# Seven block products in place of eight for the second feed-forward product of eight token groups, with a new instruction order

## The chip, the core and the metric

The kernel runs on one core of one Trainium2 chip. A core has a matrix engine (TensorE, PE in the profile, with its weight loads shown as PEld), a vector engine (VectorE, DVE), an activation engine (ScalarE, ACT), a general engine (GpSimd, POOL) and a queue engine that issues transfers (SyncE, SP). They run side by side and wait for each other through semaphores; each works through its own instructions strictly in the order in which they were written. Matrix products land in PSUM, in banks of 512 f32 values per partition; everything else is in SBUF. The metric is the device time of one execution in microseconds (us).

## What is computed

```
attention, B=4, H=8, S=768, D=64:
  keep = (column < 8) or (0 <= row - column < 96)
  scores = q k^T / 8 + (-slope[h] * distance), -1e9 where not kept
  x = softmax(scores) v, laid out as 3072 tokens x 512
feed-forward:
  h = x @ w_in                      (3072 x 2048)
  g = max(h,0) + log1p(exp(-|h|))   (softplus)
  out = g @ w_out                   (3072 x 512, f32)
```

## The kernel before

**Tiling.** The 3072 tokens are 24 blocks of 128 (`blocks`); attention works on one block `n`, the feed-forward part on a group `g` of two blocks, 256 tokens, so there are 12 groups. Matrix operands are bf16 in SBUF, sums are f32 in PSUM.

**Names of the operations.** Each step is an operation with a name, an engine, what it reads and what it writes; from these, `Program.op` (L27) derives what it waits for. For unit `i` (two blocks): `ldq/ldk/ldv` load f32 rows into a raw buffer, `castq/castk/castv` make bf16 copies, `trq/trk` transpose (on PE for units 0 to 2, by a transposing transfer from SP afterwards). For block `n`: `sc` scores (PE, L661), `z` bias (DVE, L687), `ex` exponential (ACT, L694), `pv` product with v (PE, L713), `nm` division (DVE, L724 and L725), `xt` transposition (PE or SP), `gk/gv` copies of the eight global rows. For group `g`: `a{g}.{p}`, p = 0 to 7, is product 1, eight matmuls of 256 columns (PE, L771) into one of two banks `h_ps`; `e` (ACT, L786) and `ln` (ACT, L797) make softplus into `g_t`; `b{g}.{ns}.{x}` is product 2 (PE, L820), per block `ns` 16 matmuls of 512 columns in four pieces of four; `oc` copies the PSUM bank to `osb` (DVE or ACT, L849) and `st` stores it (L852).

**Weights.** `win0` to `win7` and `wout0` to `wout7` (L429) are loads of 512 KB each of w_in and w_out; `cin` and `cout` (L431) cast them. `a{g}.6` and `a{g}.7` need the casts of win6 and win7.

**Raw buffers.** All loads share a ring of 12 raw buffers (`raw_slot`, L365), so a load waits for the casts of the load twelve places earlier. SP issues loads, transposing transfers and stores in one queue.

**Banks.** Eight: four of `s_ps`, two of `h_ps`, and `x_ps` and `o_ps` with one each. Product 2 uses `o_ps` except where `O_KEYS` and `LAST_KEYS` name another.

**What sets the order.** `ORDER` (L67) is one long list of names with their engines. It is followed as it stands: an engine gets its operations in the sequence in which they appear there. The numbers for durations and ranks at the `op` calls change nothing in what is run. `fill0` to `fill34` (L933) are 35 matmuls on zeros, whose result nothing uses.

Of the kernel before, what the change touches and what calls it, by code (L numbers as in the profile page):

```python
# [1 line left out]

# [65 lines left out]
blank:V table:A ones:G ldk0.0:S ldq0.0:A ident:G fill0:P ldk0.1:S ldq0.1:A fill1:P iota:G fill2:P ldv0:S fill3:P  # L68
ldq1.1:S dl0a:V fill4:P dl1a:V ldk1.0:S dl0b:V fill5:P dl1c:V fill6:P ldk1.1:S dl0c:V fill7:P dl1e:V d0:G fill8:P
castk0.0:A d0e:V ldv1:S fill9:P biasTrue0:V biasFalse7:A ldq1.0:S biasTrue5:V fill10:P biasTrue4:A biasTrue6:V  # L70
biasFalse3:A fill11:P biasTrue1:A win1:S biasFalse6:V castq0.1:G biasFalse5:A fill12:P win3:S castq0.0:A castk0.1:G
biasFalse1:A biasTrue3:A trq0.0:P biasFalse4:G biasTrue2:A trk0.0:P win0:S cpq0.0:A biasFalse0:G fill13:P fill14:P
cpk0.0:A fill15:P win2:S castq1.1:V fill16:P biasFalse2:A fill17:P cpq0.1:V cpk0.1:A fill18:P castk1.0:G win4:S
sb0.0:P biasTrue7:A castv0.10:V fill19:P castv0.00:G castv0.11:A sc0.0:P castk1.1:V sb1.1:P ex0.0:A sc1.1:P
castv0.01:G ex0.1:A sb1.0:P sc1.0:P ex1.1:A fill20:P pv0.0:P fill21:P ex1.0:A fill22:P castv1.00:G nm0.0:V trk1.0:P
fill23:P castq1.0:V pv0.1:P castv1.11:A fill24:P castv1.01:V pv1.1:P win5:S cpk1.0:A fill25:P nm0.1:V win7:S
trq1.0:P cpk1.1:A cin1:G nm1.1:V win6:S fill26:P fill27:P cpq1.0:A xt0:P pv1.0:P cpq1.1:A fill28:P ldk2.1:S nm1.0:V
castv1.10:A sc2.0:P ldk2.0:S xc0:A gv4.0:V fill29:P fill30:P z2.0:V xt1:P cin0:G fill31:P xc1:A z2.1:V sc3.0:P
gv4.1:A fill32:P cin3:G a0.1:P z3.0:V ex2.0:A ex2.1:A pv2.0:P cin2:G a0.0:P ldq2.1:S e0.1:A nm2.0:V ldq2.0:S ex3.0:A
gk4:G pv2.1:P sc3.1:P nm2.1:V a0.3:P e0.0:A cin4:G wout0:S z3.1:V ln0.0:A xt2:P a0.2:P cin5:G wout2:S e0.3:A xc2:V  # L80
pv3.0:P e0.2:A fill33:P a0.5:P wout1:S cin7:V ex3.1:A nm3.0:V a0.4:P e0.5:A wout3:S cin6:V pv3.1:P fill34:P e0.4:A
castk2.1:G nm3.1:V ldv2:S a0.7:P ln0.1:A castk2.0:G wout4:S a0.6:P castq2.1:V e0.7:A ln0.2:A xt3:P castq2.0:V
trk2.0:P xc3:V trq2.0:P e0.6:A a1.1:P cout0:G cpq2.0:V cpk2.0:A cpk2.1:A a1.0:P cpq2.1:V e1.1:A wout5:S cout2:V
sc4.0:P e1.0:A a1.3:P ln1.0:A z4.1:V cout1:G a1.2:P e1.3:A z4.0:V ex4.1:A b1.0.0:P ldq3:S b1.0.2:P ldk3:S a1.5:P
e1.2:A wout6:S gk5:V gv8.1:V ln1.1:A wout7:S b0.0.0:P castv2.00:G castv2.01:V sc5.0:P ex4.0:A b0.0.2:P z5.0:V a1.4:P
cout3:G ln0.3:A pv4.0:P castv2.11:G b0.0.4:P ldk4:S e1.5:A nm4.0:V sc5.1:P ldv3:S cout5:G e1.4:A b1.0.4:P z5.1:V
ex5.0:A pv4.1:P b0.0.6:P castv2.10:G b1.0.6:P gv5.0:G nm4.1:V a1.6:P castq3.0:A cout4:V b0.1.0:P gv5.1:A trq3:S
xt4:P a1.7:P castk3.11:G castk3.00:A xc4:A b0.1.2:P ex5.1:A b0.1.4:P cout6:G pv5.0:P b0.1.6:P gk6:A nm5.0:V e1.6:A
b0.0.8:P castk3.10:G ln1.2:A b0.0.10:P b0.1.8:P castk3.01:G b0.1.10:P e1.7:A cout7:G trk3:S pv5.1:P ln1.3:A
b0.1.12:P nm5.1:V b1.0.8:P b1.0.10:P castk4.00:V ldq4:S b0.0.12:P ldv4:S b0.1.14:P xt5:P castv3.11:G castv3.10:A  # L90
b1.0.12:P xc5:V castk4.01:A b1.0.14:P castk4.11:V castk4.10:A b0.0.14:P oc0.1.0:V a2.0:P gv6.0:A gv8.0:V oc0.0.0:A
st0.1.0:S a2.1:P castv3.00:V e2.0:A gk8:V oc1.0.0:V sc6.0:P e2.1:A a2.2:P castv3.01:A z6.1:V castq4.0:G b1.1.0:P
ldk5:S e2.2:A a2.3:P z6.0:V gv6.1:G st0.0.0:S ex6.1:A trk4:S a2.4:P e2.3:A gk7:G b1.1.2:P ex6.0:A trq4:S b1.1.4:P
sc7.0:P ln2.0:A ldq5:S a2.5:P z7.1:V e2.4:A pv6.0:P b1.1.6:P ldv5:S e2.5:A nm6.0:V b1.1.8:P ln2.1:A b1.1.10:P z7.0:V
# [12 lines left out]
sc12.0:P b3.1.4:P z12.0:V a4.4:P castv6.11:V castq7.0:V pv11.1:P b3.1.8:P e4.4:A z12.1:V trq7:S ln4.1:A nm11.1:V
b3.1.12:P xt11:S ex12.0:A a4.6:P ln4.0:A sc13.0:P st2.1.0:S oc3.1.0:A trk7:S a4.7:P ex12.1:A e4.6:A b4.0.0:P
st3.0.0:S e4.7:A pv12.0:P b4.0.4:P ln4.3:A nm12.0:V a5.1:P z13.1:V ln4.2:A a5.0:P e5.1:A z13.0:V b4.0.8:P ldq8:S
e5.0:A ex13.0:A pv12.1:P a5.3:P nm12.1:V b4.0.12:P xt12:S e5.3:A ex13.1:A a5.2:P oc4.0.0:V a5.5:P gk14:G ldk8:S  # L110
e5.2:A ln5.1:A pv13.0:P sc14.0:P ldv8:S nm13.0:V st4.0.0:S a5.4:P e5.5:A st3.1.0:S z14.0:V ln5.0:A pv13.1:P b4.1.0:P
nm13.1:V e5.4:A b4.1.4:P castq8.0:V xt13:S castk8.10:G castk8.11:A z14.1:V a5.6:P ex14.0:A gv14.0:G trq8:S b4.1.8:P
gv14.1:V castk8.00:G ex14.1:A b4.1.12:P gk15:A castk8.01:A a5.7:P oc4.1.0:V e5.6:A sc15.0:P castv8.10:V e5.7:A
a6.0:P b5.0.0:P ldq9:S e6.0:A ln5.2:A pv14.0:P a6.2:P nm14.0:V ln5.3:A z15.0:V a6.1:P ldk9:S pv14.1:P b5.0.4:P
e6.1:A nm14.1:V ln6.0:A a6.3:P castv8.00:V xt14:S z15.1:V e6.2:A b5.0.8:P ex15.0:A trk8:S gv15.1:V b5.0.12:P
gv15.0:V e6.3:A a6.4:P ex15.1:A oc5.0.0:V pv15.0:P castk9.01:V ln6.1:A a6.5:P nm15.0:V gk16:A castk9.00:V b5.1.0:P
castq9.0:A pv15.1:P e6.5:A b5.1.4:P nm15.1:V e6.4:A sc16.0:P gv16.0:V ln6.2:A xt15:S b5.1.8:P z16.1:V b5.1.12:P
st4.1.0:S trq9:S z16.0:V ex16.1:A a6.6:P ldv9:S a6.7:P oc5.1.0:A castk9.11:V gk17:G e6.6:A castk9.10:V gv16.1:G
# [964 lines left out]
```

## Time and profile before

| | |
|---|---|
| median of 3 runs (lowest, highest) | 216.16 us (216.04, 216.55) |
| the profiled execution: its time | 216.13 us |
| its span, first to last instruction | 214.2 us |
| PE, ACT, DVE, POOL busy | 208.3, 179.1, 117.9, 55.4 us |
| product 1 (L771), busy | 95.8 us |
| product 2 (L820) into `o_ps`, busy | 76.8 us |
| granted TensorE clock | 1.0 throughout |

The profiled execution takes 1.9 us more than its span; that lies around the span. The profile gives, for a group of instructions, the busy time, the mean length of one, and the idle time of the engine before them with what ended it. A matmul of a stream is pipelined: its own length (273 ns for 256 columns) is longer than the distance to the next, so a stream is priced from start to start.

### The profile page before, as it was taken

How to read it: one execution, taken by the hardware profiler on the slowest of the kernel's cores; microseconds unless marked ns; L12 is line 12 of the kernel's file. 1: busy time of each engine (PE TensorE's matmuls, PEld its weight loads, DVE VectorE, ACT ScalarE, POOL GpSimd, SP SyncE). 2: the span in 40 equal slices, each digit the busy share in tenths (PEclk: the TensorE clock that was granted, in tenths of full speed). 3: DMA queues.
4: the chain of work that ended last, by engine and by line, in shares of the span. 5: the costliest groups of instructions: out<-in, count | busy, mean ns of one | idle time of the engine just before them, and what ended most of it. 6: DMA issues, size and time to landing. Idle time of an engine off the chain costs nothing.

```text
span 214.2 us, 4986 instructions
## 1 busy us (share of the span) xinstructions
PE 208.3 (97%) x2003; PEld 142.3 (66%) x2003; DVE 117.9 (55%) x230; ACT 179.1 (84%) x263; POOL 55.4 (26%) x89
## 2 busy tenths in 40 slices
PE   7799999999999999999999999999999999999994
PEld 2466886657665878667767667767667666656753
DVE  5368787538587598736738575843675616300110
ACT  4999999989996998898889988998999598466651
POOL 3647435663071434300020012540043001000000
PEclk9999999999999999999999999999999999999999
DMA  5999999998999798965977679788486220300204
GB/s 190 338 378 388 387 364 341 340 230 248 239 286 194 175 233 194 178 141 167 214 194 205 67 176 230 163 215 190 135 206 78 63 98 20 105 25 3 98 0 148
DMA packets 69846, 40.95 MB, mean 191 GB/s; under 512 B 30144, under 2 KB 61248, under 8 KB 69824
## 3 DMA queue, kind: packets, MB, share of 16 engines
q1 hardware_dynamic: 69392, 40.05, 71.3%
q10 hardware_dynamic: 432, 0.59, 0.7%
q8 instruction: 15, 0.25, 0.5%
q14 instruction: 7, 0.06, 0.1%
HBM read 27.26 MB, written 6.29 MB: 157 GB/s over the span
## 4 chain that ended last, share of the span: by engine, by line
PE 90%; DMA 7%; SPq 1%; ACT 1%; POOL 0%; issue 0%
PE h_ps L771 40%; PE o_ps L820 31%; PE s_ps L820 6%; PE s_ps L661 5%; PE x_ps L713 4%; DMA raw<-in_moe_w_in_dram 4%; DMA raw<-in_v_dram 3%; PE x_ps L820 2%; SPq L388 1%; POOL w_in_bf L431 0%; PE o_ps L713 0%; PE s_ps L536 0%; ACT pb L694 0%; ACT vb L579 0%; PE o_ps L744 0%; PE x_ps L744 0%
## 5 line engine op out<-in xcount | busy, mean ns | idle before, releaser
L771 PE MATMUL h_ps<-XT,w_in_bf 128*128 128x256 bf16 x768 | 95.8, 273 | 0.0
L771 PEld LDWEIGHTS <-w_in_bf 128*128 128x128 bf16 x768 | 72.6, 98 | 17.0
L820 PE MATMUL o_ps<-w_out_bf,g 128*128 128x512 bf16 (+1 forms) x320 | 76.8, 371 | 0.0
L786 ACT ACTIVATE e<-h_ps 128x512 f32<-128x512 f32 x96 | 59.3, 630 | 15.5 <-PE h_ps L771 14.9
L820 PEld LDWEIGHTS <-g 128*128 128x128 bf16 x416 | 37.6, 98 | 29.8
L797 ACT ACTIVATE g<-e 128x1024 bf16<-128x1024 f32 x48 | 50.3, 1052 | 0.5
L687 DVE TENSOR_TENSOR z<-s_ps,biasA 128x1024 f32<-128x1024 f32 x38 | 45.7, 1219 | 6.6 <-PE s_ps L661 6.0
L694 ACT ACTIVATE pb<-z 128x1024 bf16<-128x1024 f32 (+1 forms) x44 | 43.0, 991 | 1.7 <-DVE z L687 1.5
L724 DVE RECIPROCAL rcp<-x_ps 128x4 f32<-128x4 f32 x40 | 7.2, 181 | 34.5 <-PE x_ps L713 34.2
L849 DVE COPY osb<-o_ps 128x512 f32<-128x512 f32 x13 | 9.0, 690 | 24.2 <-PE o_ps L820 24.1
L713 PEld LDWEIGHTS <-pb 128*128 128x128 bf16 x352 | 16.9, 98 | 6.1 <-ACT pb L694 0.5
L473 POOL CAST kb<-raw 64x512 bf16<-64x512 f32 x16 | 10.2, 637 | 38.8 <-DMA raw<-in_k_dram 23.5
L473 POOL CAST vb<-raw 64x512 bf16<-64x512 f32 x23 | 14.9, 646 | 15.5 <-DMA raw<-in_v_dram 13.5
L725 DVE TENSOR_TENSOR xs<-x_ps,rcp 128x256 bf16<-128x256 f32 x40 | 17.0, 424 | 1.4
L713 PE MATMUL x_ps<-vb,pb 128*128 128x65 bf16 x304 | 15.8, 193 | 0.0
L820 PE MATMUL s_ps<-w_out_bf,g 128*128 128x512 bf16 (+1 forms) x64 | 14.7, 352 | 0.0
L579 POOL COPY vb<-vb 4x512 bf16<-4x512 bf16 x12 | 7.9, 655 | 25.8 <-PE x_ps L713 25.2
L933 PE MATMUL x_ps<-blank 128*128 128x512 bf16 x35 | 11.5, 431 | 1.2 <-DVE blank L872 1.2
L661 PEld LDWEIGHTS <-kT 64*128 64x128 bf16 x224 | 6.8, 94 | 5.0 <-issue 4.9
L661 PE MATMUL s_ps<-qT,kT 64*128 64x128 bf16 x224 | 9.9, 218 | 0.0
L579 ACT COPY vb<-vb 4x512 bf16<-4x512 bf16 x10 | 6.1, 614 | 3.5 <-PE x_ps L713 3.4
L473 DVE CAST vb<-raw 64x512 bf16<-64x512 f32 x16 | 7.6, 474 | 1.1 <-DMA raw<-in_v_dram 0.8
(83 smaller groups left out, 129.7 us busy)
## 6 DMA issues: line engine op xcount, KB each, us to landing
raw<-in_v_dram SPq DMA_DIRECT2D x12, 512.0 KB, 5.6
out_dram<-osb SPq DMA_DIRECT2D x23, 256.0 KB, 2.6
raw<-in_q_dram SPq DMA_DIRECT2D x9, 512.0 KB, 4.6
raw<-in_k_dram SPq DMA_DIRECT2D x9, 512.0 KB, 5.0
raw<-in_moe_w_in_dram SPq DMA_DIRECT2D x8, 512.0 KB, 8.8
raw<-in_moe_w_out_dram SPq DMA_DIRECT2D x8, 512.0 KB, 8.1
raw<-in_k_dram SPq DMA_DIRECT2D x6, 256.0 KB, 6.3
raw<-in_q_dram SPq DMA_DIRECT2D x4, 256.0 KB, 7.6
```

The lines of the kernel that those rows point to most:

```text
L473: copy_on[eng](dst, src)
L579: copy_on[eng](vb_of(prev)[sl, :, 0:D], vb_of(first)[sl, :, 0:D])
L661: nc.tensor.matmul(reg if unit_of(n) in WIDE else reg.rearrange("p (r t) -> p r t", r=2), kt[rows, 2 * part + m, :], qv(rows, 2 * part + m ...
L687: nc.vector.tensor_tensor(z, src, bias, ALU.add)
L694: nc.scalar.activation(pb[:, 0:nr, :].rearrange("p (y a) b -> p y (a b)", y=2), src, AF.Exp, scale=1.0 / root_d)
L713: nc.tensor.matmul(xv[:, h, :], pb[:, 4 * (h % 2) + 2 * part + h // 2 if lone else u_all * (2 * (h % 2) + h // 2) + u, :], vb_of(prev if u ...
L725: nc.vector.tensor_tensor(xs[:, 4 * part : 4 * part + 4, :], xv[:, :, 0:D], rcp[:][:, :, None].to_broadcast([P, 4, D]), ALU.mult,)
L771: last = nc.tensor.matmul(hv[:, j, :], w_in_bf[:, m, fb * P : fb * P + P], XT[g % NXG][:, m, :], start=(m == 0), stop=(m == NM - 1),)
L786: nc.scalar.activation(e[:, p % 2, :, :].rearrange("p j (b t r) -> p (j b) r t", b=2, r=2), hb[:].rearrange("p (a r t) -> p a r t", a=4, r=2),
L797: nc.scalar.activation(gt[:, 2 * p - 2 : 2 * p + 2, :].rearrange("p a t -> p (a t)"), e[:].rearrange("p a j t -> p (a j t)"), AF.Ln, bias=1.0,
L820: nc.tensor.matmul(bank(key)[:, 0 : z - a], gt[:, fb, ns * P : ns * P + P], w_out_bf[:, fb, a:z], start=(fb == 0), stop=(fb == NFB - 1),)
L933: nc.tensor.matmul(x_ps[:], blank[:, 0:P], blank[:])
```

## The change

Product 2 of groups 4 to 11 is split into 2 x 2 blocks (128 tokens by 1024 features, times 1024 features by 256 outputs) and computed as Strassen's seven block products instead of eight. A11 to A22 are the four quarters of `g_t`; the sums of quarters are built on DVE or POOL (`ka`), the sums of w_out's blocks once (`ws`, 20 operations), and the seven products are put together on DVE while PSUM is emptied (`oe`). The sums of w_out read the f32 rows in the raw buffers of its one load. Eight raw buffers therefore hold w_out, two further ones are set aside, and the sums are kept in those two and in three of the eight; two more hold `ka` results. Three go back to the ring: from unit 3 on, loads go through 5 raw buffers instead of 12.

```
+FIRST_S = 4
+S_KEYS = {
+    10: {"3": ("o",), "4": ("o",), "5": ("x",), "2": ("x",), "1": ("s", 0, 0), "7": ("s", 1, 0), "6": ("s", 1, 0)},
+    11: {"3": ("o",), "4": ("o",), "5": ("x",), "2": ("x",), "1": ("s", 0, 0), "7": ("s", 1, 0), "6": ("h0",)},
+}
     def raw_slot(name):
-        raw_of[name] = len(raw_of) % NRAW
+        held = name[0] == "out"
+        if held and not spare:
+            spare.extend(idle.popleft() for _ in range(2))
+        raw_of[name] = idle.popleft()
+        if not held:
+            idle.append(raw_of[name])
...
+    def weight_sums(rank):
...
+        for p in range(4):
+            X, Y = (raw_t[at[x]][:].rearrange("p (a c) -> p a c", a=2) for x in (2 * p, 2 * p + 1))
...
+                ("6", X[:, :, lo], X[:, :, hi], ALU.add),
+                ("1", X[:, :, lo], Y[:, :, hi], ALU.subtract),
+                ("4", X[:, :, lo], Y[:, :, lo], ALU.add),
+                ("3", X[:, :, hi], Y[:, :, hi], ALU.add),
+                ("7", Y[:, :, lo], Y[:, :, hi], ALU.add),
...
+    def token_sums(g, rank):
...
+        for j, a, b in (("6", A21, A11), ("7", A12, A22), ("5", A12, A11), ("2", A21, A22), ("1", A11, A22)):
...
+                (nc.vector if eng == "DVE" else nc.gpsimd).tensor_tensor(dst, a[0], b[0], ALU.subtract)
...
+    def products(g, rank):
...
+        where = {"3": lo, "4": hi, "5": lo, "2": hi, "7": lo, "6": hi, "1": lo}
...
+            def fn(j=j, lhs=lhs, w=w):
+                for f in range(8):
+                    nc.tensor.matmul(psum(j), lhs[:, f // 2, f % 2, :], w(f), start=(f == 0), stop=(f == 7))
...
     def feed2(g):
+        if g >= FIRST_S:
+            token_sums(g, 16.0 * g + 16.0)
+            products(g, 16.0 * g + 17.0)
+            store_pair(g, 16.0 * g + 33.0)
+            return
```

`b{g}.3` to `b{g}.7` are the products, in the order 3, 4, 5, 2, 1, 7, 6 (3, 4, 5, 2, 1, 6, 7 in group 11, and 3, 5, 4, 2, 7, 6, 1 in group 10), each eight matmuls of 128 tokens by 256 columns. In groups 4 to 9 all seven use `o_ps`, two to the bank. `oe{g}.a` copies products 3 and 4 out (DVE or ACT); `oe{g}.b` is two subtractions of 256 columns, `oe{g}.c`, `.1` and `.7` are additions of 512 columns from PSUM to `osb`, in place (DVE). Group 11 has `.6` and `.7` apart, of 256 columns each, and stores its output in four quarters. `osb` becomes two buffers of 256 x 512 instead of three of 128 x 512.

`ORDER` is new as a whole, and with it the engines of many casts and copies. Of w_in and the units 1 and 2, this is the order on SP before and after:

```
-ldv0 ldq1.1 ldk1.0 ldk1.1 ldv1 ldq1.0 win1 win3 win0 win2 win4 win5 win7 win6 ldk2.1 ldk2.0 ldq2.1 ldq2.0 wout0
+ldq1.0 ldv0 ldq1.1 ldk1.0 ldk1.1 ldv1 win0 win1 win3 win2 ldq2.0 win4 win5 ldq2.1 win6 win7 ldk2.0 ldk2.1 wout0
```

The 35 `fill` matmuls stay. A stretch of the new order, with a hand-over of `o_ps` (`b4.2`, `oe4.b`, `oe4.c`, `b4.1`):

```
+e5.5:A b4.5:P z14.0:V gk15:A castk8.00:G e5.4:A b4.2:P xt13:S gv14.1:V gv14.0:G ex14.0:A a5.6:P oe4.b:V castv7.00:G
+ln5.2:A st3.1.0:S a5.7:P castk8.01:G oe4.c:V trq8:S e5.6:A castk8.11:G sc15.0:P castk8.10:V e5.7:A castv8.10:G
+pv14.0:P castv8.00:A b4.1:P castv8.11:V trk8:S ln5.3:A a6.0:P nm14.0:V ka5.6:G a6.1:P z15.1:V e6.0:A ldq9:S pv14.1:P
```

The other hunks adapt keys (`g_t` per quarter, `osb` per half) and the numbers at `op` calls, which nothing that runs depends on.

More of the change, by code (lines that the diff above doesn't have):

```diff
@@ L1 @@
 from contextlib import ExitStack
+from collections import deque
 import concourse.bass as bass
@@ L67 @@
 ORDER = """
[L68 to L82, printed above, removed]
@@ L143 @@
[L143 to L144 removed]
+blank:V ldq0.1:A iota:G ldk0.0:S fill0:P ldq0.0:A ldk0.1:S fill1:P dl0a:V fill2:P table:A ldq1.0:S dl1a:V dl0b:V
+fill3:P dl0c:V ldv0:S fill4:P dl1c:V d0:G ldq1.1:S dl1e:V fill5:P d0e:V fill6:P ldk1.0:S biasTrue4:A biasTrue7:A
+biasTrue0:V fill7:P biasFalse4:G biasTrue6:A biasTrue1:V castq0.1:A ldk1.1:S ones:G castk0.0:A biasFalse5:V ldv1:S
+ident:G biasFalse7:A biasFalse2:V biasFalse1:A win0:S castq0.0:A castk0.1:G win1:S biasFalse0:V biasTrue3:A trq0.0:P
@@ new lines, with ex @@
+    WSUM, c_t = {}, []
+    def weight_sums(rank):
+        at = {p: raw_of["out", p] for p in range(NSLOT)}
+        homes = spare + [at[0], at[1], at[2]]
+        lo, hi = slice(0, 256), slice(256, 512)
+        for p in range(4):
+            X, Y = (raw_t[at[x]][:].rearrange("p (a c) -> p a c", a=2) for x in (2 * p, 2 * p + 1))
+            xk, yk = raw_keys(at[2 * p]), raw_keys(at[2 * p + 1])
+            for z, (j, a, b, fn) in enumerate((
+                ("6", X[:, :, lo], X[:, :, hi], ALU.add),
[3 more added lines that the diff above has]
+                ("7", Y[:, :, lo], Y[:, :, hi], ALU.add),
+            )):
+                home, part = divmod(5 * p + z, 4)
+                slot = homes[home]
+                dst = raw_t[slot].bitcast(BF16)[:, 512 * part : 512 * part + 512].rearrange("p (a c) -> p a c", a=2)
+                WSUM[j, p] = dst
+                def ex(eng, dst=dst, a=a, b=b, fn=fn):
+                    (nc.vector if eng == "DVE" else nc.gpsimd).tensor_tensor(dst, a, b, fn)
+                op(f"ws{p}.{j}", "DVE", 0.0, rank, ex, reads={"6": xk, "7": yk}.get(j, xk + yk), writes=[("W", j, p)],
+                   port=True, after=[u for key in raw_keys(slot, (part // 2,)) for u in users(key)],
+                   alts={"DVE": 0.66, "POOL": 1.3})
+        for slot in (at[6], at[7]):
+            for x in range(2):
+                c_t.append((
+                    raw_t[slot].bitcast(BF16)[:, 1024 * x : 1024 * x + 1024].rearrange("p (i f t) -> p i f t", i=4, f=2),
+                    ("raw", slot, x),
+                ))
+        idle.extend((at[3], at[4], at[5]))
@@ new lines, in store_pair, with st @@
+    def store_pair(g, rank):
+        ob = osb_t[g % NOSB]
+        last = g == NGRP - 1
+        for tb, x in ((0, 1), (1, 0), (0, 0), (1, 1)) if last else ((0, None), (1, None)):
+            s, b = blocks[2 * g + tb]
+            t0 = S * s + P * b
+            cols = slice(0, DM) if x is None else slice(256 * x, 256 * x + 256)
+            queue = "ACT" if last and (tb, x) == (0, 0) else "SP"
+            def st(tb=tb, t0=t0, cols=cols, queue=queue):
+                return dma_on[queue].dma_start(out[t0 : t0 + P, cols], ob[:, tb, cols])
+            op(f"st{g}.{tb}.{x or 0}", queue, 0.4, rank, st, dma=(0.42, 60.0) if last else (0.72, 84.0),
+               reads=[("osb", g % NOSB, tb, y) for y in (range(2) if x is None else (x,))])
@@ L719, in pv @@
         reads = [("pb", at), "ones"] + v_keys(n) + (v_keys(prev) if i else [])
-        op(f"pv{n}.{part}", "PE", 0.29 if i else 0.15, rank, mm, reads=reads, writes=held([key]),
+        op(f"pv{n}.{part}", "PE", 0.237 if i else 0.12, rank, mm, reads=reads, writes=held([key]),
            count=8 if i else 4)
```

254 lines of the change are left out of this document (175 added, 79 removed).

## Prediction

> **What bounds the kernel now.** I read the page's busy times first, then the chain that ended last, then the stretches, then PE's rows by shape.
>
> ```profile
> PE 208.3 (97%) x2003; PEld 142.3 (66%) x2003; DVE 117.9 (55%) x230; ACT 179.1 (84%) x263; POOL 55.4 (26%) x89
> PE 90%; DMA 7%; SPq 1%; ACT 1%; POOL 0%; issue 0%
> ```
>
> PE is busy for 97% of the span, and 90% of the chain is PE after PE. Busy time alone proves little, since pipelined matmuls overlap, so I look at one long stretch and at the chain's pieces:
>
> ```profile
> 25.55:211.02 185.47, 185.46 (x1773) 127.94 (x1772) 102.53 (x188) 156.93 (x222) 42.10 (x64) 1.00 0.70 173
> ```
>
> ```profile
> 28.58 1.75 PE h_ps L771 x16
> 137.83 1.85 PE h_ps L771 x16
> 139.81 1.73 PE o_ps L820 x8
> ```
>
> The stretch (columns PE, PEld, DVE, ACT, POOL) shows PE without a gap from 25.55 to 211.02 us at full clock. In the chain, 16 matmuls of 256 columns take 1.75 us (0.11 each, 0.873 for an `a`), and 8 of 512 columns take 1.73 (0.216 each). Both run at one rate per column, so weight loads (98 ns in the rows by shape) hide even under 256 columns. The whole order on PE, priced like this (`sc` 0.553, `pv` 0.242, `fill` 0.216, from start to start), gives 183.1 us for this stretch against 185.5: 1.3% goes at changes between kinds of work. Hence time here is PE work, and what precedes 25.55 us.
>
> The start is bound otherwise (the timeline, then the stretches):
>
> ```profile
> 24.73 0.69 DVE L431 CAST w_in_bf<-raw 128x1024 bf16<-128x1024 f32 x1
> 25.55 1.91 PE L771 MATMUL h_ps<-XT,w_in_bf 128*128 128x256 bf16 x16
> ```
>
> ```profile
> 10.00:20.00 10.00, 9.72 (x124) 6.15 (x124) 7.24 (x18) 9.55 (x17) 6.02 (x8) 1.00 1.07 376
> 20.00:30.00 10.00, 10.00 (x121) 8.79 (x120) 7.34 (x16) 9.96 (x16) 4.88 (x7) 1.00 1.05 386
> ```
>
> `cin6` starts as win6 lands at 24.71 and ends at 25.42; `a0.7` starts 0.13 later. The DMA share is over 1 and 376 to 386 GB/s move (last columns): w_in's last load lands when all bytes queued before it have.
>
> **The change, part by part** (against the profiled execution, 216.13 us; the runs' median, 216.16, is the same to 0.03).
>
> *PE work.* Per group, 32 matmuls at 0.216 (6.91 us) become 7 x 0.873 = 6.11: 0.80 less, seven times 5.6. Group 11 had 16 x 0.216 and 16 x (0.109 + 0.056 + 0.056), 7.0 in all: 0.9 less. **-6.5 us.** A product has the shape of an `a`, so its price comes from a row.
>
> *Start.* q2, two loads of 256 KB, now stand ahead of win6 and win7. At 385 GB/s they take 2 x 0.68 = 1.36 us, so win7 lands at about 26.1 instead of 24.7; `cin7` on DVE and a hand-over end at 26.9. Ahead of `a0.7` PE has 0.45 more done (`trq2.0`), and a `fill` follows later: 1.36 - 0.45 + 0.22 = **+1.1** (bounds 0.7 and 1.7). Eight instead of 13 fillers before `trq0.0` cost nothing: PE waits for the same casts.
>
> *DVE and POOL.* New on DVE: 28 `ka`, 10 `ws`, and `oe` at 0.69 (a, like `oc`) + 2 x 0.42 (b) + 3 x 0.68 (c, 1, 7) = 3.6 per group in place of two `oc`, 1.38. On POOL: 12 `ka`, 10 `ws`, 17 more casts. The nearest rows (by shape: busy, mean ns; then by line: ns at least, median, most):
>
> ```profile
> L687 DVE TENSOR_TENSOR z<-s_ps,bias 128x512 f32<-128x512 f32 x6 | 3.9, 679 | 0.3 <-PE s_ps L661 0.3
> L687 DVE TENSOR_TENSOR z<-s_ps,biasA 128x1024 f32<-128x1024 f32 x38 | 45.7, 1219 | 6.6 <-PE s_ps L661 6.0 <-ACT e L786 0.4
> ```
>
> ```profile
> L431 DVE CAST w_in_bf<-raw x2: 694/694/694, 23.4 to 24.7; 128x1024 bf16<-128x1024 f32 x2
> L473 DVE CAST kb<-raw x12: 406/422/843, 45.8 to 158.3; 64x512 bf16<-64x512 f32 x12
> L473 POOL CAST kb<-raw x16: 607/608/862, 40.9 to 158.3; 64x512 bf16<-64x512 f32 x16
> ```
>
> `ws` on DVE has 512 elements: 0.68. `ka` has 1024 elements, all bf16: between 0.69 (the cast, as long as 512 elements of z) and 1.22 (two inputs in f32). I take 0.69, as it lies between SBUF and SBUF like the cast. On POOL a cast of 1024 takes 1.04, one of 512 0.61; two inputs lie between that and double; I take the double, 2.1 and 1.2. Sums: DVE 117.9 + 28 x 0.69 + 10 x 0.68 + 8 x 3.6 - 12 `oc` x 0.69 - 16 casts x 0.5 = about 157 us (75%); POOL 55 + 25 + 12 + 11 (casts) + 5 (`gv`) - 4 = about 104 (50%). ACT keeps its `e`, `ln`, `ex`, and stays near 179.
>
> The Trainium skill ("VectorE: DVE Perf Modes", the perf-mode tier table) lets tensor_tensor of bf16 in SBUF take two elements a cycle, and f32 one. By its formula, an estimate, `ka` would take (512 + 151) / 0.96 = 0.69 us; at 1.22 DVE's sum would be 15 us higher. No run here shows the instruction yet.
>
> *DVE held by POOL.* The cast rows show two engines in each other's way: a DVE cast takes 0.41 at best, 0.55 (k) and 0.47 (v) in the mean, and up to 0.84, longer by most of a POOL cast. Of 28, the mean excess is 0.10; POOL is busy for 26% with pieces of 0.64, so an arrival at random would wait 0.26 x 0.32 = 0.08. The model fits, and I apply it to the new order: I lay `ORDER` out along PE's priced sequence (for the kernel before this puts `sc22.0` at 164.7 us; it ran at 165.0), sum each engine over stretches of 15 us, and let every cast, `ka` and `ws` on DVE wait the mean rest of POOL's pieces. Two stretches overflow: 30 to 45 (13.0 us on DVE, 9 such instructions at 0.32: 0.8 over) and 135 to 150 (13.3, 5 at 0.43: 0.5 over). The others keep 0.4 to 9 free. **+1.3**, as z and nm queue behind and PE soon waits for them; without any hold it is 0, with twice the waits 9.5.
>
> The Trainium skill ("SBUF — State Buffer", "Who interferes with whom") speaks against the change here: a DVE instruction with two SBUF inputs and a POOL instruction that reads SBUF exclude each other, and the later one waits for the whole of the other. The cast rows agree for casts; for two inputs no row of before can show it. Without the rule for `ka` and `ws` the term would be near 0.
>
> *Hand-overs of `o_ps`.* In groups 4 to 9 PE waits four times per group for DVE (or ACT) to empty the bank; the wait stops all that follows on PE. The order puts other PE work between: 1.1 to 3.5 us. Needed are 0.9 (one `oe` and about 0.2 to pass on) or 1.7 (b and c). 24 places have enough, except the one from `b4.6` to `b5.3` (1.43 for two `gv` at 0.33 and 0.9): +0.1, counted with the next. Bounds 0 and 3, if four thin ones each meet half a POOL `ka` and more.
>
> *Loads through 5 buffers.* Loads now wait for `ws` and casts of recent loads; behind them on SP wait transposes and stores. The tightest is v3: issued at 51.6 by PE's sequence (it waits for `ws1`, which reads wout3's buffer), cast from 56.6, needed by `pv6.0` at 58.4. Landing takes 5.6 us in the median (page, v), so casts end at 58.5: **+0.1** (0 to 1.3). The other units keep 1 us and more: unit 4 is transposed at 60.9, 4 us before, and needed at 66.0.
>
> *End.* PE's last instruction is now followed by 0.42 on DVE instead of 0.27 on ACT, and a larger store: **+0.3**. DVE's own queue there: 5.9 us of work beside PE's last 6.1, so it keeps up, but a later DVE shows at once.
>
> Sum: 216.1 - 6.5 + 1.1 + 1.3 + 0.2 + 0.3 = **212.5 us**.
>
> **Rivals.** (1) *All cover holds*: no wait but the start's, 216.1 - 6.5 + 1.1 + 0.3 = 211.0. For it: PE had no gap in 185 us. Against it: DVE goes from 55% to 75%. (2) *`ka` at one element a time*, 1.22: DVE gets 0.53 more for each; the stretches overflow by 4.2 instead of 1.3, and the end's DVE queue by some 0.5: 215.9, no change. For it: both z rows run at 1.2 ns an element; against: the cast. (3) *The hold between DVE and POOL costs double*, ending slower: arrivals are not random, as both engines are released by the same events, and a POOL `ka` holds three times as long as any piece before. With twice the waits five stretches overflow, by 9.5 in all, which PE follows through z, `ex` and the hand-overs: 212.5 + 8.2 = 220.7. It decides from about 1.4 times the waits, where the overflow has eaten the other 3.6 us. Against it: most casts of before had no wait at all (median 0.42). (4) *The change doesn't do what it says*, PE's products being slower than an `a`: excluded by shape, unless strided weights matter; in the sum of (3)'s chance.
>
> **How the numbers follow.** The forecast (211.3 to 214.5) 0.58; (1) 0.12; (2) 0.12; (3) and (4) 0.18. The range holds 8 in 10 when it takes in the first three (0.82): from 210.3, (1) with the start's lower bound and a little of the 1.3% regained, to 217.0, (2) with the upper bound of the loads. A measurement tells some 0.3% (0.65 us) from no change: faster means under 215.5, which the forecast, (1) and half of (2) give: 0.76; no change 0.08, the other part of (2) and little of (3); slower 0.16.
>
> **What would show it.** PE: 2163 instructions (2003 + 448 - 288), `b` at 0.87; any gap over 0.2 us on PE belongs to a term above by its releaser. Start: `a0.7` at about 26.9. DVE at 75%, with `ka` at 0.69 if alone and 1 to 2 us when held; POOL at 50%. Stretches around 30 to 45 and 135 to 150 slower than PE's sum. The prediction fails if PE stands still in many small places (hand-overs), or if ACT, at 14.7 of 15 us busy from 30 to 45 us already, falls behind in the same stretch.

## The result, and the profile after

The changed kernel takes **213.67 us** in the median of 20 executions (212.22 to 217.63), the kernel before 216.19 in the same job (215.95 to 219.21): ratio **0.9868 [0.9848, 0.9889]**, 1.3% faster. The forecast was 212.5 us with a range from 210.3 to 217.0. Medians and ranges here are over all executions, while a ratio leaves out those that the record marks as slow, so it can differ a little from the quotient of the medians. In the profiled execution of the changed kernel (215.54 us, span 213.6) the record of the granted clock has it at one half for 3.41 us near the start; four of the 20 executions have such a mean clock (0.990 to 0.992). Where later waits are counted, I therefore use the run called `control`, the same kernel once more (profiled execution 213.30 us, span 211.4).

The page of the changed kernel, busy times and the chain that ended last:

```profile
PE 202.9 (95%) x2149; PEld 159.8 (75%) x2163; DVE 158.3 (74%) x289; ACT 177.8 (83%) x257; POOL 107.3 (50%) x127
PE 81%; DVE 7%; issue 4%; ACT 3%; DMA 2%; POOL 1%; ACTq 0%; POOLq 0%; DVEq 0%
```

Weight loads show the 2163 instructions of PE that were forecast (14 records of matmuls are missing), DVE stands at 74% (forecast 75%) and POOL at 50% (50%). The chain is new: PE's part fell from 90% to 81%, and DVE, issue, ACT and POOL, which had 1% or less, hold 15%. The end is still set by PE, but PE now stops for others.

The groups of the new instructions (busy us, mean ns | idle before them): L512 are the products, L447 `ka`, L412 `ws`:

```profile
L512 PE MATMUL o_ps<-raw,raw 128*128 128x256 bf16 x144 | 17.8, 272 | 0.0
L447 POOL TENSOR_TENSOR raw<-g 128x1024 bf16<-128x1024 bf16 x8 | 17.0, 2130 | 23.3 <-ACT g L982 17.7 <-ACT vb L764 3.4 <-PE o_ps L512 2.1
L447 DVE TENSOR_TENSOR raw<-g 128x1024 bf16<-128x1024 bf16 x16 | 10.9, 688 | 3.0 <-ACT g L982 1.7 <-PE o_ps L512 0.7 <-PE s_ps L512 0.6
L447 DVE TENSOR_TENSOR g<-g 128x1024 bf16<-128x1024 bf16 x12 | 9.0, 758 | 0.7 <-POOL raw L447 0.5
L412 POOL TENSOR_TENSOR raw<-raw 128x512 bf16<-128x512 f32 x4 | 5.1, 1270 | 0.1
L412 DVE TENSOR_TENSOR raw<-raw 128x512 bf16<-128x512 f32 x4 | 2.7, 685 | 0.1
```

A matmul of a product has 272 ns, as one of an `a` has (273), and waits 0.0 us: no extra for strided weights, and nothing lost at the hand-overs of `o_ps`. `ka` takes 0.69 us on DVE (the mean of 16; the other twelve have 0.76, one of them being held), not 1.22, and 2.13 on POOL. The timeline's last PE rows put a product at 0.87 us from start to start:

```profile
207.74 1.04 PE L512 MATMUL s_ps<-raw,raw 128*128 128x256 bf16 x8
208.61 1.04 PE L512 MATMUL h_ps<-raw,raw 128*128 128x256 bf16 x8
209.49 1.04 PE L512 MATMUL s_ps<-raw,raw 128*128 128x256 bf16 x8
```

So the saving was as worked out, and the question is what took back 3.7 of the 6.5 us (216.13 - 6.5 - 213.30 = -3.7 in `control`). PE has exactly the same operations ahead of `b1.0.0` in both kernels (groups 0 and 1 of product 1, the first attention blocks), one filler aside. So its start splits the loss: 32.57 us before, 34.29 in `control`, **1.7 us lost at the start** and the other 2.0 behind it.

The 1.7 us are not a wait for loads. PE's first real work, `trq0.0`, starts at 6.89 us before and at 6.65 in `control`; from there to `b1.0.0` PE takes 25.68 us and 27.64, with 0.2 and 0.3 us of listed idle time. It has more to do, or does it more slowly: the rows at the start, shown below, are slow, and four fillers more stand behind `trq0.0` in the new order (26 against 22 ahead of `b1.0.0`; 4 x 0.216 = 0.9 us). From `a0.3` to `b1.0.0` alone it is 11.68 us before and 13.07 in `control`, with no listed wait in either: six fillers and `pv2.1`, ahead of `a0.3` in the old order, stand behind it in the new one.

Behind `b1.0.0` the kernel before has no wait on PE that its view of waits lists; `control` has (34 to 209 us; in total, times, longest):

```profile
PE h_ps L954 <- ACT e L969: 0.6, 2, 0.4
PE s_ps L844 <- DMA kTa<-kb: 0.5, 1, 0.5
PE o_ps L1001 <- issue: 0.2, 1, 0.2
```

The first line is `a3.2` (0.45) and `a7.1` (0.18), the second `sc12.0`. For `a7.1` the view names `e`, but `xt15`, which it needs too, landed at 127.70 us, 0.14 before its start.

(In the kernels of the experiments a line stands two earlier than in the changed kernel: `a` is L954, products L510; where an edit made `ORDER` a line longer, one earlier.)

The start, in the timeline of PE, first the kernel before, then the changed one:

```profile
6.89 0.62 PE L536 MATMUL s_ps<-ident,qb 128*128 128x128 bf16 x8 [1.25 <-POOL qb L449]
7.44 0.62 PE L536 MATMUL s_ps<-ident,kb 128*128 128x128 bf16 x8
9.20 0.60 PE L598 MATMUL h_ps<-bias,ident 128*128 128x256 bf16 x4
```

```profile
7.11 0.62 PE L721 MATMUL s_ps<-ident,qb 128*128 128x128 bf16 x8 [2.52 <-ACT qb L634]
7.57 0.95 PE L721 MATMUL s_ps<-ident,kb 128*128 128x128 bf16 x8
8.74 1.06 PE L783 MATMUL h_ps<-bias,ident 128*128 128x256 bf16 x4
```

and the changed kernel's stretch from 7.68 to 11.09 us (the third column from the right is the granted clock):

```profile
7.68:11.09 3.41, 3.41 (x24) 1.87 (x22) 2.35 (x4) 2.38 (x6) 1.19 (x2) 0.50 1.09 358
```

The wait for the first cast of q grew from 1.25 to 2.52 us, as five fillers less stand in front of it, and 0.6 us later the clock goes to one half: the `sb` row (`h_ps<-bias`) takes 1.06 instead of 0.60. In `control` the same rows are as slow, although the view shows a clock of 1.00 there:

```profile
6.65 1.03 PE L719 MATMUL s_ps<-ident,qb 128*128 128x128 bf16 x8 [1.87 <-ACT qb L632]
7.48 1.06 PE L719 MATMUL s_ps<-ident,kb 128*128 128x128 bf16 x8
8.76 1.06 PE L781 MATMUL h_ps<-bias,ident 128*128 128x256 bf16 x4
```

The trace's record of the clock begins at 4.22 us in the kernel before, at 4.27 in the changed one and only at 10.18 in `control`; ahead of that the view's 1.00 stands for no record, so "1.0 throughout" in the table of the kernel before holds from 4.22 us on. The fillers ahead of these times start 0.43 us apart, and where more follow, as in the kernel before, those behind 0.21 to 0.22. So in every profile PE starts at half its rate. In the first profile of the changed kernel the clock rose, PE waited, and the clock fell again; in `control` it rose only after the wait.

### The profile page after: what moved, and what is told of

Same layout as the page of the kernel before. It is cut to its first block, busy times and chain, and to the rows that moved or that the text cites. A ratio compares the mean times of both kernels' runs of the same rounds, so it can differ in the third digit from the quotient of the medians.

```text
span 213.6 us, 5384 instructions
## 1 busy us (share of the span) xinstructions
PE 202.9 (95%) x2149; PEld 159.8 (75%) x2163; DVE 158.3 (74%) x289; ACT 177.8 (83%) x257; POOL 107.3 (50%) x127
## 4 chain that ended last, share of the span: by engine, by line
PE 81%; DVE 7%; issue 4%; ACT 3%; DMA 2%; POOL 1%; ACTq 0%; POOLq 0%; DVEq 0%
PE h_ps L956 37%; PE o_ps L512 18%; PE o_ps L1003 6%; PE s_ps L846 5%; PE x_ps L898 4%; PE s_ps L1003 3%; DMA raw<-in_q_dram 2%; PE x_ps L1116 2%; DVE z L872 2%; ACT e L971 2%; PE x_ps L512 1%; DVE vb L658 1%; PE s_ps L512 1%; PE s_ps L721 1%; DVE xs L910 1%
## 5 line engine op out<-in xcount | busy, mean ns | idle before, releaser
L447 POOL TENSOR_TENSOR raw<-g 128x1024 bf16<-128x1024 bf16 x8 | 17.0, 2130 | 23.3 <-ACT g L982 17.7
L512 PEld LDWEIGHTS <-g 128*128 128x128 bf16 x256 | 24.6, 98 | 2.9
L1003 PE MATMUL o_ps<-w_out_bf,g 128*128 128x512 bf16 x87 | 22.5, 379 | 0.6 <-issue 0.2
L658 POOL CAST kb<-raw 64x512 bf16<-64x512 f32 x24 | 15.6, 652 | 14.1 <-DMA raw<-in_k_dram 9.0
L512 PEld LDWEIGHTS <-raw 128*128 128x128 bf16 x192 | 18.4, 98 | 2.0
L1003 PEld LDWEIGHTS <-g 128*128 128x128 bf16 x128 | 11.5, 98 | 10.8
L764 POOL COPY vb<-vb 4x512 bf16<-4x512 bf16 x20 | 12.3, 616 | 11.2 <-PE x_ps L898 10.7
L512 PE MATMUL o_ps<-raw,raw 128*128 128x256 bf16 x144 | 17.8, 272 | 0.0
L634 POOL CAST qb<-raw 128x1024 bf16<-128x1024 f32 (+1 forms) x12 | 11.7, 972 | 10.5 <-DMA raw<-in_q_dram 10.4
L512 PE MATMUL o_ps<-raw,g 128*128 128x256 bf16 x128 | 15.9, 273 | 0.0
L447 POOL TENSOR_TENSOR g<-g 128x1024 bf16<-128x1024 bf16 x4 | 8.8, 2204 | 9.1 <-DVE raw L447 8.9
```

The costliest lines, as they stand in the source:

```text
L447: (nc.vector if eng == "DVE" else nc.gpsimd).tensor_tensor(dst, a[0], b[0], ALU.subtract)
L512: nc.tensor.matmul(psum(j), lhs[:, f // 2, f % 2, :], w(f), start=(f == 0), stop=(f == 7))
L658: copy_on[eng](dst, src)
L764: copy_on[eng](vb_of(prev)[sl, :, 0:D], vb_of(first)[sl, :, 0:D])
L1003: nc.tensor.matmul(bank(key)[:, 0 : z - a], gt[:, fb, ns * P : ns * P + P], w_out_bf[:, fb, a:z], start=(fb == 0), stop=(fb == NFB - 1),)
```

## Experiments

Two theories of the loss, named C and H in the first expectations: **C**, at the start PE stands idle too long without its five fillers, and the clock falls (or, as the rows of `control` have it, rises late); **H**, behind it VectorE and GpSimd hold each other. The first four kernels ran on one chip against the kernel before.

**1. control.** The changed kernel again.

> The changed kernel once more, without an edit. It gives a second trace. If the waits on PE seen in the first trace (1.2 us ahead of sc5.1 near 39 us, 1.8 us in two steps between 74 and 78 us) come from the order, they are here again at the same operations; if they were chance, they are elsewhere. Its time should be 213.3 +- 0.7 us.

Measured: 213.41 us (212.44 to 216.63), ratio 0.9861 [0.9841, 0.9880]: the result repeats. The waits do so only in part. The one ahead of `sc5.1` (1.02 us idle in the first profile) is absent; of the two steps between 74 and 78 us (0.79 and 0.65) only `a3.2` is left, with 0.45.

**2. before_fewer_fill.** The kernel before, with 8 fillers ahead of `trq0.0` instead of 13.

```
-fill8:P fill9:P fill10:P fill11:P fill12:P trq0.0:P
-FILLERS = 35
+trq0.0:P
+FILLERS = 30
```

> The kernel before, with five of the 13 fill matmuls ahead of trq0.0 left out (30 in all), nothing else. Theory C: the granted clock falls to 0.5 somewhere between 7 and 12 us in some executions, and a0.7 comes up to 1 us later, time 216.2 to 217. Rival: PE's work there has room, a0.7 hangs on win6 at 24.7 us, and the time stays at 216.2.

Measured: 217.86 us (217.09 to 218.95), ratio 1.0078 [1.0057, 1.0099], more than the 217 that was expected at most. Its record has the clock at one half from 7.53 to 10.95 us; `a0.3` starts at 22.73 instead of 20.89, `a0.7` at 27.38 instead of 25.55 and `b1.0.0` at 34.39 instead of 32.57. Five matmuls on zeros, which nothing uses, are worth 1.65 us to the kernel before.

**3. more_fill.** The other way round: five fillers more in the changed kernel, 13 ahead of `trq0.0`.

```
-trq0.0:P
-FILLERS = 35
+fill8:P fill9:P fill10:P fill11:P fill12:P trq0.0:P
+FILLERS = 40
```

> The changed kernel with five more fill matmuls ahead of trq0.0 (13 there, as before the change; 40 in all). Theory C: the first trace shows the granted clock at 0.5 from 7.68 to 11.09 us, since PE stands idle from 4.4 to 7.1 us; with 13 fillers the clock stays at 1.0, PE reaches a0.7 some 0.5 to 1.3 us earlier, and the times scatter less: 212.5 us. Rival: the start waits for loads and DVE only, PE has time to spare, and the time stays at 213.3; the five fillers themselves would then cost 0.

Measured: 214.14 us (213.93 to 214.30), ratio 0.9902 [0.9889, 0.9915]. C is half right. The clock is at full from 4.56 us on, and from the start of `trq0.0` to the first product of q and k PE takes 2.24 us instead of 3.53 in `control`. All four executions lie within 0.4 us, `a0.3` starts at 20.51 instead of 21.21, `a0.7` at 27.03 instead of 27.72 and `b1.0.0` at 33.60 instead of 34.29. Yet the time is not shorter but 0.4% longer than in `control`: what follows `b1.0.0` takes 1.5 us more. The waits of PE behind 34 us say where most of that went:

```profile
PE h_ps L954 <- DMA XT<-xs: 1.3, 2, 1.0
PE s_ps L844 <- DMA kTa<-kb: 0.7, 1, 0.7
PE h_ps L954 <- ACT e L969: 0.3, 1, 0.3
PE o_ps L1001 <- issue: 0.2, 1, 0.2
```

PE comes earlier to `a7.1`, `a9.0` and `sc12.0`, and the transposing DMAs behind which they stand gain less, or nothing: `xt15` is issued 0.5 us earlier than in `control` and lands 0.3 later (128.03 against 127.70), as the load of v9 ahead of it takes 5.9 us instead of 4.2. That was in neither theory, and why the same load takes longer there no run shows.

**4. unhold.** For H: `castv2.10` from DVE to POOL, `ws3.3` and `ws3.4` from POOL to DVE at a later place.

```
-castv2.10:V  ... ws3.4:G  ... ws3.3:G
+castv2.10:G  ... oc2.1.0:V ws3.4:V  ... gk11:V ws3.3:V
```

> The changed kernel with three moves: castv2.10 from DVE to POOL, ws3.4 and ws3.3 from POOL to DVE and to a place some 7 and 13 us later. Theory H (DVE waits while POOL reads): the two long waits of PE, 1.2 us at 39 us and 1.8 us at 74 to 78 us, go, since the DVE casts that took 1.38 and 2.72 us (0.41 alone) no longer stand behind a POOL sum; time 213.3 - 2 to 3 = 210.5 to 211.3. Rival D (DVE is late because of its own load): DVE gets 0.9 us more work, the waits stay or move, time 213 to 214.

Measured: 212.86 us (211.78 to 214.56), ratio 0.9824 [0.9800, 0.9848]. In the profile the wait of `a3.2` at 74 us is gone (the one at 39 us is absent in `control` too). The time lies between the theory's and the rival's, and the interval overlaps with that of `control`, so the time alone proves no gain. The profiled execution starts late, `b1.0.0` at 35.94 us: its record of the clock begins at 12.79.

**5 to 8.** On another chip: four kernels on the base of `more_fill`, whose executions lie close together.

```
fill_q2late: ldq2.0, ldq2.1 behind win7; their casts, transposes and copies later
fill_xt:     -xt14 behind ldv9   +xt14 ahead of st4.1.0   -ldv9 +ldv9 behind xt15
             -xt19 behind ldk11  +xt19 ahead of ldk11     -ldv7 +ldv7 behind trk6
fill_all:    both, and unhold's edit
fill_nosums: no ka, no ws
```

> Against the kernel with 13 fillers ahead of the first transpose (214.1 us, a0.7 at 27.0, win7 landed 26.2): the two 256 KB loads of q2 go behind win7 again, where the kernel before had them. My start term says that they cost 1.1 us: win7 should land at about 25.0 and a0.7 start at 25.9. Theory 'the start is the loads': 213.0 to 213.3 us. Rival 'it is given back later': a0.7 is early, but the chains that are not the product engine's own (transposing DMAs, sums on VectorE and GpSimd) stand at their own times, and it stays at 213.8 to 214.3 us.

> Against the kernel with 13 fillers ahead of the first transpose (214.1 us): four transposes of the SyncE queue (xt14, xt19, and those that stand behind a v load) are issued ahead of the load or store that stood before them. The waits of a7.1 (1.16 us on XT), a9.0 (0.47) and sc12.0 (0.82 on kTa) should shrink by half or more. Theory 'those DMA waits are what the early start was lost to': 212.0 to 212.6 us. Rival 'waits on VectorE, ScalarE or GpSimd stand right behind them': 213.6 to 214.2 us.

> The two edits above together, on 13 fillers, with the cast castv2.10 given to GpSimd and ws3.3 and ws3.4 to VectorE at a later place. If the three gains add: 214.1 - 1.0 - 1.8 - 0.6 = 210.7 us, range 210.3 to 211.5. If the first two are two names for one slack: 212 to 213 us.

> Against the kernel with 13 fillers ahead of the first transpose (214.1 us): all 48 sums of activations (ka) and all sums of w_out (ws) are left out, the products read quarters and blocks that were not summed, so the output is not the reference's. It takes 37 us of VectorE's and GpSimd's work away and changes no transfer and no matmul. Theory 'the sums and the holds that they make cost the later waits': 212.0 to 212.6 us. Rival 'the later waits are the transposing DMAs': 213.7 to 214.2 us.

Measured: `fill_q2late` 215.08 us (one of its six executions took 422), ratio 0.9929 [0.9913, 0.9946]; `fill_xt` 217.73, 1.0036 [1.0008, 1.0064]; `fill_all` 217.39, 1.0033 [1.0001, 1.0065]; `fill_nosums` 213.32, 0.9862 [0.9827, 0.9897]. None came out as its theory had it. The first three are slower than theory and rival alike, two of them by far: moves meant to gain lost up to 1.4% against `more_fill`. `fill_nosums` (40 `ka` left out, not the 48 that its expectation names) lies between its theory and its rival; it keeps the wait of `a7.1` for `xt15` (0.96 us), which the sums therefore don't make. The transposes of `fill_xt` did come early, as the DMA view of 116 to 131 us shows (kind, number, median us from issue to landing), first `more_fill`, then `fill_xt`:

```profile
XT<-xs SPq DMA_TRANSPOSE x2, 6.1
```

```profile
XT<-xs SPq DMA_TRANSPOSE x2, 2.7
```

But in `fill_xt` PE and ACT stand still right there:

```profile
127.59 0.41 PE L896 MATMUL x_ps<-vb,pb 128*128 128x65 bf16 x8
130.10 3.15 PE L954 MATMUL h_ps<-XT,w_in_bf 128*128 128x256 bf16 x14 [2.10 <-ACT e L969]
```

```profile
128.78 0.62 ACT L656 CAST vb<-raw 64x512 bf16<-64x512 f32 x1 [2.92 <-DMA raw<-in_v_dram]
129.42 1.15 ACT L969 ACTIVATE e<-h_ps 128x512 f32<-128x512 f32 x2
```

```profile
130.20:133.20 3.00, 3.00 (x15) 2.13 (x15) 1.48 (x3) 2.60 (x4) 1.55 (x2) 0.50 0.00 0
```

A chain of four links, none of which is the transpose: the load of v9, now behind `xt15`, lands at 128.75 instead of 126.45; `castv9.11`, which nothing needs before block 18, stands in ACT's queue ahead of `e6.7` and waits for it; PE waits 2.10 us for the bank that `e6.7` empties; and after this wait the clock is at one half for 3.41 us. In the same way DVE waits 2.39 us for v7 in `castv7.01`, ahead of `z12.0`. In `fill_xt`, the seven executions with a mean clock of 0.992 took 217.5 to 218.5 us, the five with 0.999 or 1.0 took 215.7 to 216.8: one fall of the clock costs about 1.9 us. `more_fill` has the same chain, only shorter: there ACT waits 1.46 us in that cast, which ends at 127.09, and `xt15` lands at 128.03, 0.13 before `a7.1` starts.

In `fill_q2late`, win7 lands at 24.71 instead of 26.15, but `a0.7` starts only 0.5 us earlier, as `cin7` waits on DVE behind the norm `nm3.0`; and `cpq2.1`, ahead of `e0.6` on ACT, waits for q2, so that `a1.0` loses 0.8. Again an operation that uses a load that had become later stood in front of old work.

**9 and 10. fill_xt_casts and fill_xt_casts_unhold.** `fill_xt` with five casts of v7 and v9 moved behind the work that they held; then `unhold`'s edit on top.

```
-castv9.11:A ahead of e6.7   +e7.0:A castv9.11:A
-castv9.01:G                 +castk9.01:G castv9.01:G
-castv7.01:V ahead of z12.0  +z12.1:V castv7.01:V
-castv7.11:A ahead of e4.5   +ln4.0:A castv7.11:A
-castv7.10:G                 +castk7.11:G castv7.10:G
```

> Against the kernel with 13 fillers (214.1 us) and against the one with the four transposes ahead of the loads (217.7 us): the transposes stay ahead, and the casts of the loads that became later (v7 and v9) stand behind the score sums of group 12 and the drains of pair 7 that they held: castv9.11 behind e7.0 on ScalarE, castv9.01 behind castk9.01 on GpSimd, castv7.01 behind z12.1 on VectorE, castv7.11 behind ln4.0 on ScalarE, castv7.10 behind castk7.11 on GpSimd. Theory 'the slowdown came from casts that stood in front and waited for a later load, and the 2.1 us wait that they made took the clock down': a7.1 waits under 0.6 us, sc13.0 no longer, the recorded clock stays 1.0, and the time is 211.8 to 212.8 us. Rival 'transposes and loads share the engines, so that early transposes cost later loads as much': 213.5 to 215 us.

> The kernel above, with castv2.10 on GpSimd and the two sums ws3.3 and ws3.4 on VectorE at a later place. Theory 'VectorE and GpSimd hold each other at 39 and 74 us whatever the later transposes do': a3.2 waits under 0.2 us (0.49 without it) and the time is 0.4 to 0.8 us under that of the kernel above. Rival 'what is gained at 74 us is waited off at the next transposes': within 0.2 us of it.

Measured: `fill_xt_casts` 212.50 us (212.05 to 213.25), ratio **0.9820 [0.9799, 0.9842]**: 2.2% less than `fill_xt` from five moved casts (0.9820 / 1.0036 = 0.978). Part of that is the clock: against the five executions of `fill_xt` without a fall (median 215.88 us, 0.9971 of the kernel before) it is 1.5%. Against `control` it is 0.4%, with intervals that just overlap. The rival, that transposes and loads must pay for each other (213.5 to 215 us), falls. Of the waits of PE between 34 and 209 us one line is left:

```profile
PE h_ps L954 <- ACT e L969: 0.7, 1, 0.7
```

That is `a3.2` at 74 us, the one of H. With `unhold`'s edit this line goes too, but the time, 212.58 us, 0.9831 [0.9800, 0.9862], does not become shorter: the expected gain of 0.4 to 0.8 us isn't shown. The rival's time is met, but not its cause, as no later wait is listed. In the profile, the stretch from `b1.0.0` to PE's last product is 0.54 us shorter (172.21 against 172.75), and the start of that execution 0.4 later.

**11 and 12. fill_xt_casts_q2 and fill_xt_casts_nosums.** On that base the start again, with `cpq2.1` behind `e0.6` and `cin7` ahead of `nm3.0`; and the sums again.

```
fill_xt_casts_q2:     fill_q2late's edit, +e0.6:A cpq2.1:A  +cin7:V nm3.0:V
fill_xt_casts_nosums: no ka, no ws
```

> Against the kernel with the transposes ahead and the casts behind (212.5 us, a0.7 at 26.9): q2's two loads behind win7 as in the kernel before, and this time nothing of theirs stands in front of older work: the copy cpq2.1 behind the drain e0.6 on ScalarE, and the cast cin7 ahead of the norm nm3.0 on VectorE. Theory 'the place of q2's loads costs the 1.1 us that the prediction gave the start': a0.7 at 25.6 to 26.0, no wait of a1.0, 211.3 to 211.7 us. Rival 'the start is set by the score chain and not by the loads': a0.7 under 26.5 but the time within 0.3 us of 212.5.

> The kernel with the transposes ahead and the casts behind (212.5 us), without any of the sums of activations and of w_out, so that the products read quarters and blocks that were not summed and the output is not the reference's. Theory 'sums cost what VectorE and GpSimd hold each other, 1.3 us by the prediction': 211.0 to 211.4 us. Rival 'only the one wait at 74 us was theirs': 211.8 to 212.1 us. A third, 'with the transposes early the sums cost nothing': 212.3 to 212.7 us.

Measured: `fill_xt_casts_q2` 213.32 us, 0.9865 [0.9840, 0.9891]: no gain, and slower than theory and rival. The casts of the last load and the rows of PE, first `fill_xt_casts`, then this one:

```profile
26.06 0.69 DVE L614 CAST w_in_bf<-raw 128x1024 bf16<-128x1024 f32 x1 [0.29 <-DMA raw<-in_moe_w_in_dram]
26.93 1.04 PE L954 MATMUL h_ps<-XT,w_in_bf 128*128 128x256 bf16 x8
33.50 0.59 PE L1001 MATMUL o_ps<-w_out_bf,g 128*128 128x512 bf16 x2
```

```profile
24.48 0.69 DVE L615 CAST w_in_bf<-raw 128x1024 bf16<-128x1024 f32 x1 [0.70 <-DMA raw<-in_q_dram]
26.25 1.04 PE L955 MATMUL h_ps<-XT,w_in_bf 128*128 128x256 bf16 x8
33.47 0.59 PE L1002 MATMUL o_ps<-w_out_bf,g 128*128 128x512 bf16 x2
```

`cin7` is 1.6 us earlier, `a0.7` 0.7, and `b1.0.0` (the last row) 0.03. In neither kernel does PE wait for a load between `a0.3` and `b1.0.0`; it is simply not through. Between `a0.3` and `a0.7` the new order has 8 fillers where the order before had 2 (6 x 0.216 = 1.3 us), and `pv2.1` besides. `a0.7` gains 0.7 us because `trq2.0` (0.45) now stands behind it and `a0.3` starts 0.23 earlier; `trq2.0` has to be done before `b1.0.0` all the same. The load is close, though: in `fill_xt_casts` its cast ends at 26.75, 0.2 us before `a0.7`. Loads and PE's own sequence reach this point almost together, so undoing one of them returns nothing.

`fill_xt_casts_nosums` 212.40 us (211.24 to 212.66), 0.9801 [0.9775, 0.9828]: 0.2% less, which the intervals don't tell from nothing, and by its time the third case, that the sums cost nothing. In its profile PE has no wait over 0.2 us behind 34 us, and its stretch from `b1.0.0` to the last product is 171.99 us against 172.75: all sums together (28 us of DVE's work and 39 of POOL's by the groups of the page, more than the 37 that the expectations name) cost about the one wait of `a3.2`, 0.76 us.

The profiled executions side by side. "Behind" is the time from the start of `b1.0.0` to that of PE's last product, and "waits" the sum of PE's listed waits between 34 and 209 us.

| kernel | fillers first | `b1.0.0` | behind | waits | median | ratio |
|---|---|---|---|---|---|---|
| control | 8 | 34.29 | 172.94 | 1.3 | 213.41 | 0.9861 |
| more_fill | 13 | 33.60 | 174.43 | 2.5 | 214.14 | 0.9902 |
| unhold | 8 | 35.94 | 172.54 | 0.7 | 212.86 | 0.9824 |
| fill_xt | 13 | 33.20 | 177.95 | 4.3 | 217.73 | 1.0036 |
| fill_nosums | 13 | 34.29 | 173.49 | 1.7 | 213.32 | 0.9862 |
| fill_xt_casts | 13 | 33.50 | 172.75 | 0.7 | 212.50 | 0.9820 |
| fill_xt_casts_nosums | 13 | 34.10 | 171.99 | 0.0 | 212.40 | 0.9801 |

"Behind" less the waits is 171.6 to 172.1 us in all rows but `fill_xt`, where the fall of the clock adds 1.9: what the kernels lose behind `b1.0.0` is these waits. The starts scatter more: `b1.0.0` comes at 33.20 to 34.29 us in the profiles with 13 fillers and the same order of loads, at 34.29 to 35.94 in those with eight.

## Why the forecast was near, step by step

The forecast has 2.9 us of losses, the profile of `control` 3.7. The terms of DVE and of the end were too high, those of the start and of the loads too low, so that their errors partly cancel: that the sum came so near is in part luck.

- **PE work, -6.5 us: right.** 2163 instructions, a product at 0.87 us, 0.0 us of waits before its rows. This term is over five times the error of the sum (1.2 us), and carried the forecast.
- **Start, +1.1: near in size, wrong in cause, and the step "Eight instead of 13 fillers before `trq0.0` cost nothing" failed.** win7 did land at 25.8 to 26.2 us as worked out, but `a0.7` does not hang on it: in `control` `cin7` is done at 27.16, and `a0.7` starts at 27.72, straight behind `trq2.0`. The six fillers and `pv2.1` behind `a0.3`, which I had not counted there, keep PE busy up to `b1.0.0`, and with q2's loads put back that start gained 0.03. What it loses is time of PE's own sequence: four fillers more behind `trq0.0` (0.9 us by their price; no run takes them out) and, with eight ahead of it, 1.3 us at half clock (3.53 us against 2.24 in `more_fill`). That 1.1 came out near 1.0 (33.60, with 13 fillers) to 1.7 (34.29, with eight) is luck. In the kernel before, the five fillers are worth 1.65 us in the runs. I asked only what PE waits for, the same cast, and not what the wait does to PE's clock. No run has eight fillers together with the moved transposes and casts, so what the five are worth there is not shown.
- **DVE held by POOL, +1.3: too high.** Without any sums the stretch behind `b1.0.0` is 0.94 us shorter on `more_fill` and 0.76 on `fill_xt_casts`. Arrivals are not random, but to the good side: in `control`, casts, `ka` and `ws` on DVE ran 7.0 us over their shortest in all, where the model (a mean rest of POOL's piece for every instruction) amounts to 18.7. Of the 28 `ka` only one took over 0.72 us. The sum doesn't matter, the place does: in `control` only this one, `castv5.01` beside `ws3.3`, reached PE: behind it stood `z9.1`, and behind `ex9.1` on ACT the `e` that empties the bank `a3.2` waits for:

```profile
70.16 1.56 DVE L656 CAST vb<-raw 64x512 bf16<-64x512 f32 x1
...
70.17 1.26 POOL L410 TENSOR_TENSOR raw<-raw,raw 128x512 bf16<-128x512 f32 x1
```

  In `unhold`, where `ws3.3` and `ws3.4` are elsewhere, this cast takes 0.52 us and the wait is gone. Of the Trainium skill's rule ("SBUF — State Buffer", "Who interferes with whom"), that DVE's second port pair and GpSimd exclude each other, the runs bear out that it holds for two inputs: in `control` a `ka` that met a cast of q on POOL with 0.98 us still to go took 1.52 us instead of 0.68. The rule agrees with the trace, and its price here is small.
- **Loads through 5 buffers, +0.1: the step that failed behind the start; measured 1.0 in `control`, 2.4 in `more_fill`.** I compared each load's landing with the block that needs its data, and found 1 us of slack and more. For v9 that is so; but two other things hang on a load's place: the transposes behind it on SP (`xt14`, `xt15`, `trk6`, `xt19`; for the first two 5.3 us in `control` and 6.1 in `more_fill` instead of 2.7), and whatever stands behind its casts in the queues of ACT and DVE. v9's data are needed at block 18, v9's cast stands ahead of `e6.7`.
- **Hand-overs, +0.1: about 0,** as forecast. **End, +0.3: -0.1;** from PE's last instruction to the end of the span 3.12 us (3.21 before).
- **The rivals.** `ka` at 1.22 us is excluded by its row (0.69). Doubled holds are excluded by 7.0 us against 18.7 (and a POOL `ka` is twice, not three times, the longest cast of before, 1.04 us). "All cover holds", 211.0, misses by the start and the late transposes, and by DVE only with `a3.2`.

Sum of `control` by the runs: 216.1 - 6.5 + 1.7 (start) + 0.6 (`a3.2`) + 1.0 (`sc12.0` 0.67, `a7.1` 0.34) - 0.1 (end) = 212.8, against 213.3; the rest of 0.5 lies in pieces under 0.25 us that no run here tells apart. (The waits are counted here from start to start, which adds 0.16 us to each listed idle time.) Still open is how far the scatter of the changed kernel (212.2 to 217.6) is all the clock's: its four executions at a mean clock of 0.990 to 0.992 took 215.2 to 217.6 us, the others, but for one, 212.2 to 214.5. But a clock that rises late, as in `control`, does not show in this mean.

## What to carry to other kernels

Price a load not only by when its data are needed, but by what stands behind its cast in an in-order queue: a cast of data needed 18 us later can stop the engine that everyone waits for now, and moving five such casts gave 2.2% here, the clock's fall included. Where an order is rewritten, compare the idle time of the matrix engine ahead of its first real work with that in the old order, and count fillers as work that moves: they bring the clock up in one place and are the bound in another. When a repaired start brings nothing, look for the first later wait that stands at its own time.

## What the runs showed of the hardware

The matrix engine starts at half its rate: fillers are 0.43 us apart up to 4.22 us in the kernel before and 0.22 from there on. The record of the clock begins with this rise (3.99 to 12.79 us in these profiles), and a view of a stretch ahead of it shows 1.00 all the same; the length of the rows tells the difference (1.06 us against 0.60).

After an idle time the clock can fall back to one half, for 3.41 us in each of the three falls recorded near the start or at `a7.1`. An idle time of 2.5 us (the changed kernel, `trq0.0`), 2.3 (`before_fewer_fill`) or 2.1 (`fill_xt`, `a7.1`) was enough; after 2.1 us in the profile of `fill_all`, 1.25 in that of the kernel before and 1.15 in that of `more_fill` it did not fall. The Trainium skill ("TensorE: Matmul & The Clock Gate", "Part 1: The HAM clock gate") has it that the clock falls after an idle window of about 3.4 us, and that the windows run free of the kernel's start. The length agrees with 3.41 us. The idle time does not have to fill a window by these rows, and 2.1 us on either side of the fall would fit windows that run free, which no run here shows by itself.

Transposing DMAs issued behind a load of 512 KB took 5.3 us (`control`) and 6.1 (`more_fill`), those issued ahead of it 2.7 (`fill_xt`).
